# First copies of q and k on VectorE, and a new step order, in a one-core attention and two-layer kernel

## The chip, the cores and the metric

The kernel runs on one core of one Trainium2 chip. The time is that of the device for one execution, in microseconds (us); each kernel's figure is the median of several runs.

## The reference

```python
scores = scale * np.matmul(q, k.transpose(0, 1, 3, 2))   # q, k, v: 2 x 12 heads x 448 x 64
scores = np.where(np.triu(np.ones((448, 448), bool), k=1), -1e9, scores)
scores = scores - scores.max(-1, keepdims=True)
attn = np.exp(scores)
attn = attn / (attn.sum(-1, keepdims=True) + 1e-9)
x = np.matmul(attn, v)              # then heads side by side: x is 896 x 768
h = x @ w_in                        # 768 x 2048
x = np.maximum(0.01 * h, h) @ w_out # 2048 x 768
xn = x / np.sqrt(np.mean(x * x, -1, keepdims=True) + 1e-6) * rms_g
g, val = xn @ w_gate, xn @ w_val    # 768 x 1536 each
out = (g / (1 + np.exp(-g)) * val) @ w_out2
```

## The kernel before

The first 97 us or so are the attention, the rest is a long row of matrix products of the two layers. The attention works on 12 pairs of heads. For each pair p the steps are, by their names in the table `ORDER`: load k and q (`k`, `q`), turn them with TensorE (`tk`, `tq`, lines 306 and 309), take them out of PSUM in a high part (`hk`, `hq`, line 315) and a low part (`lk`, `lq`, line 319), multiply scores (`s`, line 345: blocks 0, 1, 4, 5, then 2, 3, then the tail block 6), take the mask and the row peak (`m`, line 354, VectorE), the exponential (`e`, line 363, ScalarE), guard and inverse of the sums (`g`, `i`), normalise (`n`, line 376), turn the probabilities (`t`, line 383), copy them out (`c`, line 396), multiply by the values (`x`, line 405) and copy the result out in two parts (`f`, lines 413 and 415).

Pair 0 is handled in pieces: its q and k come in chunks a, b and c, are turned on line 269, copied on line 275 and multiplied in plain float32 (line 331, steps `s0.0` to `s0.6`). The q chunks of pair 0 are loaded by DMAs that ScalarE's own queue issues (line 263); all other loads go through SP's queue, in the order of the table. `b`, `d` and `v` load the tails of q, of v, and v itself.

`ORDER` is a written list: each engine gets its instructions in that order and works them off in that order. A mark `@A`, `@D` or `@P` says ScalarE, VectorE or GpSimd where a step can be done by more than one; without a mark a copy goes to VectorE and a normalisation to GpSimd. `~3` is three small multiplies on constants (line 516), which do no work of the result. `w` decodes the first weights of the layers, `y` multiplies the first layer's first columns for the first batch already inside the attention, `z` finishes them.

Buffers rotate: four PSUM banks for scores, three for everything that is turned, one for the value product, four tiles for loaded q and k. A step that takes a bank waits until the last reader of the bank's former content is through.

```python
            def copy_part(p, nm, part, eng):
                (ACT.copy if eng == "A" else DVE.tensor_copy)(
                    out=L["F", p][:, 0, at:at + n].bitcast(F32), in_=L["ps" + nm + part, p][:, :n])
```

Of the kernel before, what the change touches and what calls it, by code (L numbers as in the profile page):

```python
# [15 lines left out]
P = 128  # L16
B, H, S, D = 2, 12, 448, 64
# [20 lines left out]


ORDER = """  # L40
k0a q0a k0b q0b k0c q0c k1 q1 b0 tk0a hk0a@A tq0a hq0a@D ~3 s0.0 tk0b hk0b@A tq0b hq0b@D m0.0 m0.1 e0.0 tk0c
hk0c@A ~1 tq0c hq0c@D s0.2 e0.1 tk1 k2 hk1@A m0.3 m0.2 g0.0@D i0.0 s0.4 q2 q3 b2 lk1 tq1 e0.2 e0.3 hq1@A s0.6
m0.5 m0.4 k3 lq1 e0.5 m0.6 g0.2@P e0.4 tk2 ~1 s1.2 hk2@A s1.0 tq2 i0.2 g0.4@D k4 n0.3@P e0.6 i0.4 m1.2 n0.4@P
lk2 s1.6 e1.2 m1.0 m1.4 g0.6@P hq2@A m1.3 i0.6 lq2 e1.4 n0.5@P n0.2@P tq3 t0.1 e1.0 hq3@A c0.1@A m1.6 tk3
n0.6@P s2.0 n0.1@P n0.0@P hk3@A m1.5 m1.1 lq3 d0 q4 lk3 e1.1 e1.3 e1.5 s2.2 m2.4 m2.1 m2.0 t0.0 m2.2 m2.5
c0.0@A m2.3 e1.6 g1.0@D t0.3 t0.2 s2.6 i1.0 c0.3@A tk4 n1.0 n1.6@P e2.3 c0.2@A m2.6 e2.6 e2.4 s3.0 n1.1 hk4@D
m3.4 n1.4@D e2.0 e2.5 s3.2 tq4 m3.0 m3.2 hq4@D lk4 v0 n1.3 t1.3 lq4 e2.2 e3.4 e2.1 n1.2 n1.5@P x0 c1.3@D t1.0
b1 t1.1 g2.0@P e3.0 c1.0@D m3.1 t1.2 q5 k6 k5 f0.0@A c1.1@A c1.2@A m3.5 m3.3 s3.6 q7 w0.0 i2.0 m3.6 tk6 tq5
f0.1 n2.0 e3.5 hk6@A lk6 q6 tk5 s4.0 e3.1 hk5@A hq5@A n2.6@P s4.2 e3.6 e3.2 m4.0 lq5 m4.3 n2.5@P m4.1 n2.4@P x1
n2.3 e3.3 n2.2 n2.1 lk5 m4.4 g3.0@P w0.1@P e4.1 t2.3 t2.0 t2.2 m4.5 e4.0 i3.0 c2.0@D c2.2@D c2.3@A m4.2 s4.6  # L50
t2.1 q8 e4.3 tq7 tq6 f1.0@A hq7@A c2.1@A n3.1 n3.2 n3.0 n3.6@P s5.0 f1.1 e4.2 m4.6 s5.2 e4.6 e4.5 e4.4 x2
n3.4@P n3.3 hq6@D lq6 lq7 n3.5@P m5.0 m5.4 m5.1 t3.0 t3.3 k7 v1 c3.0@A m5.3 g4.0@D s5.6 t3.2 i4.0 c3.3@A e5.4
e5.1 n4.5@D n4.3 m5.5 m5.2 f2.0@A c3.2@D t3.1 n4.1 tk7 c3.1@A hk7@A m5.6 e5.6 d1 n4.4@P e5.2 s6.0 e5.0 e5.5
n4.0 n4.6@P s6.2 f2.1 m6.4 w0.2 e5.3 m6.0 n4.2 x3 lk7 m6.1 t4.3 w0.3 g5.0@P t4.0 c4.3@A i5.0 f3.0@A m6.2 m6.5
k8 w1.0 v2 c4.0@A s6.6 t4.1 n5.6@P n5.3 m6.3 t4.2 n5.2 n5.5@P n5.1 k9 c4.1@D f3.1 e6.5 c4.2@A s7.6 tk8 tq8 s7.0
e6.0 n5.4@P n5.0 w1.1@P m6.6 m7.6 s7.2 e6.4 hq8@D x4 e6.2 q9 hk8@D m7.0 lk8 lq8 e6.3 t5.0 e6.1 e7.0 t5.2 e6.6
m7.3 m7.4 t5.1 s8.6 g6.0@P c5.2@D f4.0@A c5.0@A e7.6 c5.1@A i6.0 t5.3 m7.2 m7.1 m7.5 c5.3@A tq9 tk9 n6.4@P
hk9@A e7.4 f4.1 m8.6 e7.5 s8.0 hq9@D n6.6@P n6.3 m8.0 m8.5 lq9 k11 q10 s8.2 n6.5@P e7.1 e7.2 n6.2 n6.1 n6.0
e8.0 x5 lk9 m8.2 m8.4 t6.3 e7.3 m8.1 g7.0@D f5.0@A i7.0 q11 t6.0 c6.3@A t6.1 c6.0@A e8.1 k10 w0.4 m8.3 n7.4@P
w0.5@P n7.5@P c6.1@A t6.2 c6.2@A e8.3 s9.0 n7.0 f5.1 m9.0 m9.4 e8.6 m9.5 e8.4 s9.2 n7.1 e8.5 e8.2 e9.5 m9.1 x6  # L60
tk11 s9.6 tq10 n7.2 w0.6 m9.3 hq10@A y0.0 tk10 g8.0@P n7.3 hk11@D m9.2 i8.0 lk11 n8.6@P n8.3 y0.1 t7.0 n7.6@P
hk10@A e9.4 c7.0@A lq10 lk10 y0.2 m9.6 t7.2 f6.0@D t7.3 tq11 y0.3 e9.0 e9.6 c7.2@A v3 t7.1 n8.5@D s10.6 c7.3@D
t8.3 n8.1 w1.2 e9.2 hq11@A c7.1@D e9.3 c8.3@A y0.4 lq11 n8.0 n8.2 n8.4@P t8.0 w1.3 t8.1 t8.2 e9.1 c8.1@A c8.0@A
w1.4 m10.6 g9.0@P f6.1 i9.0 y0.5 n9.5@D n9.1 n9.0 s10.0 z0.0 e10.6 c8.2@A m10.1 m10.0 n9.2 n9.3 m10.5 w1.5@A
s10.2 e10.0 m10.4 m10.3 m10.2 x7 f7.0@A s11.2 n9.4@P e10.2 f7.1 e10.1 e10.4 e10.5 w1.6 s11.0 e10.3 m11.3 m11.5
m11.4 g10.0@P x8 n9.6@P i10.0 m11.2 t9.1 t9.0 f8.0@A c9.1@D f8.1 t9.2 y1.0 m11.0 c9.0@D e11.5 n10.1 n10.4@P
n10.0 n10.5@P t9.3 s11.6 n10.6@D m11.1 t10.0 e11.2 e11.4 n10.2 e11.3 c9.2@A e11.1 z0.1 w2.0 y1.1 g11.2@P n10.3
c9.3@D t10.3 e11.0 i11.2 m11.6 n11.3@D g11.4@D t10.2 n11.2@P i11.4 g11.0@P y1.2 e11.6 x9 n11.4@D c10.2@D
g11.6@D c10.0@A n11.5@P w2.1@A c10.3@D f9.0@A i11.6 t11.2 t10.1 c11.2@A c10.1@A n11.6@D t11.3 y1.3 i11.0 f9.1
n11.0@P n11.1@P w2.2 x10 f10.0@A t11.1 t11.0 c11.1@A y1.4 y1.5 c11.0@A w2.3 z0.2 f10.1 c11.3@D x11 z1.0 f11.0@A  # L70
w2.4 f11.1 z1.1 z1.2
"""


# [613 lines left out]
```

## Time and profile before

| | us |
|---|---|
| median of 3 runs | 589.68 (589.5 to 589.83) |
| the profiled execution, its own time | 591.89 |
| span from its first to its last instruction | 590.1 |
| TensorE busy in that span | 585.5 |
| VectorE busy | 390.0 |
| ScalarE busy | 265.9 |
| GpSimd busy | 47.6 |

The profiled execution is a single one; its span is what the trace covers, its own time includes what lies around the span. A busy TensorE is not TensorE at its peak: the ends of its multiplies are modelled, and a multiply that runs at half the clock, or waits inside its pipeline, counts as busy too.

### The profile page before, as it was taken

The numbers are of one execution on the slowest core, as the hardware profiler recorded it, in microseconds if no ns is written. First come the engines' busy times: TensorE is split into PE (matmuls) and PEld (weight loads), VectorE is DVE, ScalarE is ACT, GpSimd is POOL, SyncE is SP. The second block draws the span as 40 slices with busy tenths as digits, with TensorE's granted clock in tenths as the row PEclk, the third lists the DMA queues.
The fourth block names the chain that finished last, engine by engine and source line by source line (L and its number), as shares of the span: only waits on it lengthen the run. The fifth ranks groups of instructions, "written<-read, shape, count | busy, mean of one in ns | idle before, by whom it ended". The sixth has DMA issues, their size and how long they took to land.

```text
span 590.1 us, 8451 instructions
## 1 busy us (share of the span) xinstructions
PE 585.5 (99%) x3267; PEld 533.6 (90%) x3267; DVE 390.0 (66%) x706; ACT 265.9 (45%) x520; POOL 47.6 (8%) x104
## 2 busy tenths in 40 slices
PE   9999999999999999999999999999999999999997
PEld 5878878999999999999999999999999999999997
DVE  5999996766666555655655998788797796850000
ACT  4989894444444434323333743434444444420000
POOL 3465550000000000000000000000000000000000
PEclk9999999999999999999999999999999999999999
DMA  5893413333333333334233354334343351621001
GB/s 133 204 216 80 96 54 107 108 110 109 109 109 111 112 100 98 108 94 139 91 107 111 105 160 139 116 124 147 115 152 120 108 159 55 190 78 41 28 27 41
DMA packets 83448, 65.04 MB, mean 110 GB/s; under 512 B 35536, under 2 KB 80336, under 8 KB 83408
## 3 DMA queue, kind: packets, MB, share of 16 engines
q1 hardware_dynamic: 82448, 64.27, 37.0%
q8 instruction: 26, 0.43, 0.3%
q10 hardware_dynamic: 960, 0.23, 0.2%
q14 instruction: 14, 0.11, 0.1%
HBM read 61.74 MB, written 2.75 MB: 109 GB/s over the span
## 4 chain that ended last, share of the span: by engine, by line
PE 99%; ACTq 0%; ACT 0%; issue 0%
PE mm L545 17%; PE mm L153 10%; PE mm L154 10%; PE mm L155 10%; PE mm L564 7%; PE mm L563 7%; PE mm L562 7%; PE mm L643 5%; PE mm L645 5%; PE mm L644 5%; PE pt L383 4%; PE x L405 4%; PE s L345 4%; PE qk L306 2%; PE s L331 1%; PE mm L422 0%
## 5 line engine op out<-in xcount | busy, mean ns | idle before, releaser
L153 PE MATMUL mm<-a,hi 128*128 128x448 f32 x300 | 109.7, 366 | 0.0
L154 PE MATMUL mm<-a,lo 128*128 128x448 f32 x300 | 109.6, 365 | 0.0
L155 PE MATMUL mm<-a,hi 128*128 128x448 f32 x300 | 109.6, 365 | 0.0
L134 ACT CAST hi<-we 128x768 fp32r<-128x768 f32 (+1 forms) x59 | 48.2, 817 | 132.0 <-PE mm L545 53.9
L140 DVE TENSOR_TENSOR lo<-we,hi 128x768 fp32r<-128x768 f32 (+1 forms) x60 | 56.0, 933 | 64.5 <-ACT hi L134 64.3
L123 DVE SCALAR_TENSOR_TENSOR we<-we,ws 128x768 int32<-128x768 int32 (+1 forms) x70 | 65.4, 935 | 28.5 <-ACT we L112 26.4
L545 PE MATMUL mm<-a,hi 128*128 128x448 f32 x336 | 81.7, 365 | 0.0
L112 ACT ACTIVATE we<-raw 128x768 f32<-128x768 f32 (+1 forms) x68 | 60.3, 888 | 39.4 <-DVE lo L140 26.0
L545 PEld LDWEIGHTS mm<-a,hi 128*128 128x128 f32 x336 | 63.1, 188 | 5.0
L127 DVE SCALAR_TENSOR_TENSOR we<-raw,we 128x768 int32<-128x768 int32 (+1 forms) x70 | 65.1, 931 | 1.4
L562 PE MATMUL mm<-b,hi 128*128 128x448 f32 x168 | 61.4, 365 | 0.0
L564 PE MATMUL mm<-b,lo 128*128 128x448 f32 x168 | 61.4, 365 | 0.0
L563 PE MATMUL mm<-b,hi 128*128 128x448 f32 x168 | 61.4, 365 | 0.0
L153 PEld LDWEIGHTS mm<-a,hi 128*128 128x128 f32 x300 | 56.3, 188 | 4.5
L154 PEld LDWEIGHTS mm<-a,lo 128*128 128x128 f32 x300 | 56.3, 188 | 4.5
L155 PEld LDWEIGHTS mm<-a,hi 128*128 128x128 f32 x300 | 56.3, 188 | 4.5
L545 PE MATMUL mm<-a,lo 128*128 128x448 f32 x168 | 47.7, 365 | 0.0
L363 ACT ACTIVATE p<-p,st 128x256 f32<-128x256 f32 (+3 forms) x84 | 44.2, 538 | 0.9 <-DVE st L354 0.5
L119 DVE TENSOR_SCALAR ws<-raw 128x768 int32<-128x768 uint32 (+1 forms) x70 | 38.0, 543 | 8.0 <-DMA raw<-in_moe_w_gate_dram 3.3
L376 POOL TENSOR_SCALAR p<-p,st 128x256 f32<-128x256 f32 (+3 forms) x76 | 37.6, 513 | 20.1 <-DVE st L372 6.6
L656 DVE COPY o<-mm 128x384 f32<-128x384 f32 x6 | 3.3, 555 | 53.0 <-PE mm L645 53.0
L563 PEld LDWEIGHTS mm<-b,hi 128*128 128x128 f32 x168 | 31.6, 188 | 2.5
(136 smaller groups left out, 944.0 us busy)
## 6 DMA issues: line engine op xcount, KB each, us to landing
raw<-in_moe_w_out_dram SPq DMA_DIRECT2D x24, 768.0 KB, 4.3
raw<-in_moe_w_in_dram SPq DMA_DIRECT2D x16, 768.0 KB, 4.7
raw<-in_moe_w_gate_dram SPq DMA_DIRECT2D x12, 768.0 KB, 4.4
raw<-in_moe_w_val_dram SPq DMA_DIRECT2D x12, 768.0 KB, 4.3
raw<-in_moe_w_out_dram SPq DMA_DIRECT2D x6, 512.0 KB, 3.6
out_dram<-o SPq DMA_DIRECT2D x14, 192.0 KB, 1.9
n<-in_k_dram SPq DMA_DIRECT2D x22, 112.0 KB, 2.8
vn<-in_v_dram SPq DMA_DIRECT2D x12, 192.0 KB, 4.1
```

The lines of the kernel that those rows point to most:

```text
L112: ACT.activation(out=out, in_=src, func=AF.Copy, scale=2.0 ** -112)
L123: DVE.scalar_tensor_tensor(out=L["e"], in0=L["e"], scalar=3, in1=L["s"], op0=ALU.logical_shift_left, op1=ALU.bitwise_or)
L127: DVE.scalar_tensor_tensor(out=L["e"], in0=L["w"][:, :, 1], scalar=-0x80000000, in1=L["e"], op0=ALU.bitwise_and, op1=ALU.bitwise_or)
L134: ACT.copy(out=L["hi"], in_=L["e"].bitcast(F32))
L140: DVE.tensor_tensor(out=L["lo"], in0=L["e"].bitcast(F32), in1=L["hi"].bitcast(F32), op=ALU.subtract)
L153: PE.matmul(ps, wh, ah, start=(i == 0), stop=False)
L154: PE.matmul(ps, wl, ah, start=False, stop=False)
L155: PE.matmul(ps, wh, al, start=False, stop=(i == n - 1))
L545: PE.matmul(pss[b], w, cols(xT[kk], b)[part], start=kk + part == 0 and w is wh, stop=kk == KC - 1 and w is wl)
L562: PE.matmul(pss[b], wh, ah, start=(f == 0), stop=False)
L563: PE.matmul(pss[b], wh, al, start=False, stop=False)
L564: PE.matmul(pss[b], wl, ah, start=False, stop=(f == NF1 - 1))
```

## The change

Only `ORDER` is different. In its first row the step `hk0a`, the copy of k's chunk a, loses the mark `@A` and so goes to VectorE; `hq0a` was on VectorE already. From `s0.0` on the steps are in a new order, with some of the marks different. One of the small multiplies on constants (`~1` ahead of `s1.2`) is gone. Everything else in the program is the same; all line numbers behind the table are lower by one. The diff, cut to the first rows:

```diff
 ORDER = """
-k0a q0a k0b q0b k0c q0c k1 q1 b0 tk0a hk0a@A tq0a hq0a@D ~3 s0.0 tk0b hk0b@A tq0b hq0b@D m0.0 m0.1 e0.0 tk0c
-hk0c@A ~1 tq0c hq0c@D s0.2 e0.1 tk1 k2 hk1@A m0.3 m0.2 g0.0@D i0.0 s0.4 q2 q3 b2 lk1 tq1 e0.2 e0.3 hq1@A s0.6
-m0.5 m0.4 k3 lq1 e0.5 m0.6 g0.2@P e0.4 tk2 ~1 s1.2 hk2@A s1.0 tq2 i0.2 g0.4@D k4 n0.3@P e0.6 i0.4 m1.2 n0.4@P
-lk2 s1.6 e1.2 m1.0 m1.4 g0.6@P hq2@A m1.3 i0.6 lq2 e1.4 n0.5@P n0.2@P tq3 t0.1 e1.0 hq3@A c0.1@A m1.6 tk3
...
+k0a q0a k0b q0b k0c q0c k1 q1 b0 tk0a hk0a tq0a hq0a ~3 s0.0 tk0b hk0b@A tq0b hq0b@D m0.0 m0.1 e0.0 tk0c hk0c@A
+~1 tq0c e0.1 hq0c@D s0.2 tk1 hk1@A m0.2 m0.3 s0.4 g0.0@D tq1 s0.6 q2 e0.3 e0.2 lk1 hq1@A m0.4 e0.4 m0.5 e0.5 k2
+lq1 g0.2@P tq2 hq2@A m0.6 s1.2 i0.2 g0.4@D n0.3@P i0.0 i0.4 k3 s1.0 e0.6 m1.2 n0.2@P n0.5@P n0.4@P tk2 tk3 s1.6
+d0 m1.3 lq2 n0.0@P e1.2 e1.3 m1.1 m1.0 hk2@A m1.5 hk3@A n0.1@P g0.6@P e1.5 t0.1 lk2 b2 m1.4 lk3 q3 m1.6 i0.6
+n0.6@P k4 e1.0 e1.4 s2.6 e1.1 e1.6 q4 m2.6 t0.0 tq3 c0.1@A hq3@D g1.0@D i1.0 n1.6@P s2.0 s2.2 c0.0@A t0.3
...
```

Over the whole list VectorE has 3 large casts of q or k fewer and 1 copy of probabilities fewer, 3 normalisations more and 2 first parts of `f` more.

The first place is the start of VectorE's list. `F_147` is the tile of pair 0 that holds its turned k and q, `qk_145` and `qk_149` are the turned chunks a of k and of q, `qk_162` is chunk b of q. Before:

```order
L498 MEMSET qe_96 128x1536
L275 COPY F_147<-qk_149 128x128
L275 COPY F_147<-qk_162 128x128
L354 ISA p_98,st_165<-s_155,mask_102 128x128
L354 ISA st_165 128x1
```

And of the change:

```order
L497 MEMSET qe_96 128x1536
L274 COPY F_147<-qk_145 128x128
L274 COPY F_147<-qk_149 128x128
L274 COPY F_147<-qk_162 128x128
L353 ISA p_98,st_165<-s_155,mask_102 128x128
```

VectorE's list has one copy more, at its head; the same copy is gone from ScalarE's list, where it stood right behind the load of the activation table.

The second place is TensorE's list from the turned q of pair 1 on; `s<-F 64x448` is `s0.6`, rows of 112 columns are k, of 128 columns q. Before:

```order
L309 MATMUL qk<-ident,qe 128x128
L331 MATMUL s<-F 64x448 x2
L306 MATMUL qk<-ident,n 128x112 x4
L516 LDWEIGHTS const-bfloat16-1.0
L516 MATMUL warm<-const-bfloat16-1.0 128x256
L345 MATMUL s<-F 128x256 x6
L345 MATMUL s<-F 128x128 x6
L345 MATMUL s<-F 128x384 x6
L306 MATMUL qk<-ident,n 128x128 x3
L309 MATMUL qk<-ident,qe 128x128
L345 MATMUL s<-F 128x448 x3
L306 MATMUL qk<-ident,n 128x128 x3
```

And of the change:

```order
L330 MATMUL s<-F 64x448 x2
L305 MATMUL qk<-ident,n 128x128 x3
L308 MATMUL qk<-ident,qe 128x128
L344 MATMUL s<-F 128x256 x6
L344 MATMUL s<-F 128x128 x6
L344 MATMUL s<-F 128x384 x6
L305 MATMUL qk<-ident,n 128x112 x8
L344 MATMUL s<-F 128x448 x3
L382 MATMUL pt<-ident,p 128x128 x4
L344 MATMUL s<-F 128x448 x3
L382 MATMUL pt<-ident,p 128x128 x4
L305 MATMUL qk<-ident,n 128x128 x3
```

Pair 2's q is turned first and its k later, together with pair 3's k; the tail scores of pair 2 (the second `128x448`) moved ahead of its other scores.

The third place is VectorE's list of the change in front of those tail scores. `F_226` is pair 2's tile: the row with 512 columns is `lq2`, that with 448 is `lk2`; `st_260` belongs to pair 1.

```order
L318 TENSOR_TENSOR F_188<-qk_197,F_188 128x512
L353 ISA p_98,st_165<-s_202,mask_tail_103 128x448
...
L353 ISA p_98,st_260<-s_229,mask_102 128x256
L353 ISA p_98,st_260<-s_230,mask_102 128x256
L318 TENSOR_TENSOR F_226<-qk_221,F_226 128x512
L353 ISA p_98,st_260<-s_246,mask_102 128x128
L353 ISA p_98,st_260<-s_245,mask_102 128x128
L353 ISA p_98,st_260<-s_246,mask_102 128x384
L318 TENSOR_TENSOR F_226<-qk_265,F_226 128x448
```

Before, `lk2` stood right behind the first peak of pair 1, ahead of six others and of `lq2`; now it is behind five of those peaks and behind `lq2`.

## Rows read from the trace of the kernel before

**Rows 1.** TensorE's waits: engine, line, what ended them; us, times, longest.

```profile
PE s L331 <- ACT F L275: 0.4, 1, 0.4
```

**Rows 2.** Chain of waits up to 35 us: start, us, engine, tile and line.

```profile
4.64 0.80 PE s L331 x4
...
9.30 1.58 PE s L331 x4
10.88 0.83 PE qk L306 x3
...
11.93 0.92 PE s L331 x4
12.85 0.54 PE qk L306 x4
...
13.49 1.50 PE s L345 x18
15.00 0.48 PE qk L306 x3
...
15.58 0.60 PE s L345 x3
16.18 0.33 PE qk L306 x3
16.51 0.11 PE qk L309
...
17.59 1.41 PE s L345 x18
19.00 1.46 PE pt L383 x12
...
23.94 1.88 PE x L405 x16
```

**Rows 3.** Timeline from 2.9 us: start, us, engine, line, operation, tiles.

```profile
2.94 0.66 PE L269 MATMUL qk<-ident,n 128*128 128x128 f32 x2
...
3.02 1.28 ACT L275 ACT_TABLE_LOAD   x1 [3.02 <-issue]
...
3.39 0.84 PE L516 MATMUL warm<-const-bfloat16-1.0 128*128 128x256 bf16 x3
...
3.63 0.29 DVE L275 COPY F<-qk 128x128 f32<-128x128 f32 x1 [1.18 <-PE qk L269]
```

**Rows 4.** Timeline of VectorE from 12 us.

```profile
12.58 0.69 DVE L319 TENSOR_TENSOR F<-qk,F 128x512 fp32r<-128x512 f32 x1 [0.61 <-ACT F L315]
13.19 0.61 DVE L354 CUSTOM_DVE_ANT_0 p<-s,mask_tail 128x448 f32<-128x448 f32 x1
...
14.08 0.42 DVE L354 CUSTOM_DVE_ANT_0 p<-s,mask 128x256 f32<-128x256 f32 x1
...
14.43 0.62 DVE L319 TENSOR_TENSOR F<-qk,F 128x448 fp32r<-128x448 f32 x1
14.96 0.28 DVE L354 CUSTOM_DVE_ANT_0 p<-s,mask 128x128 f32<-128x128 f32 x1
...
15.17 0.55 DVE L354 CUSTOM_DVE_ANT_0 p<-s,mask 128x384 f32<-128x384 f32 x1
```

**Rows 5.** Costliest groups: the exponentials; busy us, mean ns, idle before.

```profile
L363 ACT ACTIVATE p<-p,st 128x256 f32<-128x256 f32 (+3 forms) x84 | 44.2, 538 | 0.9 <-DVE st L354 0.5
```

**Rows 6.** Timeline of SP's queue from 6.5 us.

```profile
6.64 1.07 SPq L253 DMA_DIRECT2D n<-in_k_dram  x2
7.81 0.97 SPq L253 DMA_DIRECT2D n<-in_q_dram  x2
```

**Rows 7.** Windows: PE, PEld, DVE, ACT, POOL busy us (instructions), clock, DMA.

```profile
40.00:60.00 20.00, 20.00 (x184) 16.32 (x184) 18.79 (x67) 18.83 (x60) 10.92 (x23) 1.00 0.57 115
```

**Rows 8.** Timeline around the value product of pair 8.

```profile
78.51 0.62 DVE L415 TENSOR_TENSOR a<-x,a 128x448 fp32r<-128x448 f32 x1 [0.61 <-ACT a L413]
...
79.24 0.60 PE L405 MATMUL x<-pT,vn 128*64 128x448 f32 x2
```

More of the change, by code (lines that the diff above doesn't have):

```diff
@@ L40 @@
 ORDER = """
-k0a q0a k0b q0b k0c q0c k1 q1 b0 tk0a hk0a@A tq0a hq0a@D ~3 s0.0 tk0b hk0b@A tq0b hq0b@D m0.0 m0.1 e0.0 tk0c
-hk0c@A ~1 tq0c hq0c@D s0.2 e0.1 tk1 k2 hk1@A m0.3 m0.2 g0.0@D i0.0 s0.4 q2 q3 b2 lk1 tq1 e0.2 e0.3 hq1@A s0.6
-m0.5 m0.4 k3 lq1 e0.5 m0.6 g0.2@P e0.4 tk2 ~1 s1.2 hk2@A s1.0 tq2 i0.2 g0.4@D k4 n0.3@P e0.6 i0.4 m1.2 n0.4@P
-lk2 s1.6 e1.2 m1.0 m1.4 g0.6@P hq2@A m1.3 i0.6 lq2 e1.4 n0.5@P n0.2@P tq3 t0.1 e1.0 hq3@A c0.1@A m1.6 tk3
-n0.6@P s2.0 n0.1@P n0.0@P hk3@A m1.5 m1.1 lq3 d0 q4 lk3 e1.1 e1.3 e1.5 s2.2 m2.4 m2.1 m2.0 t0.0 m2.2 m2.5
@@ L46 @@
[L46 to L70, printed above, removed]
@@ L71 @@
-w2.4 f11.1 z1.1 z1.2
+k0a q0a k0b q0b k0c q0c k1 q1 b0 tk0a hk0a tq0a hq0a ~3 s0.0 tk0b hk0b@A tq0b hq0b@D m0.0 m0.1 e0.0 tk0c hk0c@A
[3 more added lines that the diff above has]
+n0.6@P k4 e1.0 e1.4 s2.6 e1.1 e1.6 q4 m2.6 t0.0 tq3 c0.1@A hq3@D g1.0@D i1.0 n1.6@P s2.0 s2.2 c0.0@A t0.3
@@ new lines @@
+c0.3@A m2.0 lq3 v0 t0.2 m2.4 c0.2@A m2.5 t1.3 tq4 tk4 m2.1 m2.2 n1.2 e2.0 n1.0 m2.3 n1.4@D hk4@D s3.0 s3.2
+n1.5@P n1.1 n1.3 k5 e2.5 e2.1 e2.3 hq4@A m3.3 lq4 m3.2 m3.0 lk4 x0 q5 k6 e2.6 c1.3@A t1.1 t1.2 e2.2 m3.4 e2.4
+g2.0@D c1.2@D f0.0@A t1.0 s3.6 m3.1 c1.1@A c1.0@A tk6 tk5 m3.5 tq5 m3.6 i2.0 f0.1 e3.0 e3.5 e3.1 e3.6 hq5@A
+s4.0 q7 n2.3 n2.4@P n2.0 e3.4 hk5@A s4.2 x1 hk6@D m4.4 lk6 w0.0 m4.2 lk5 b1 n2.2 n2.6@P n2.5@P n2.1 lq5 q6 e3.3
+m4.0 t2.3 k7 f1.0@D v1 q8 e4.2 e3.2 g3.0@P t2.1 c2.3@A t2.2 c2.1@A i3.0 m4.5 s4.6 c2.2@A e4.4 m4.3 t2.0 tq7 tq6
@@ new lines @@
+f1.1 n3.3 m4.1 s5.0 m4.6 hq7@A c2.0@A n3.4@P n3.6@P lq7 m5.4 m5.5 hq6@A s5.2 e4.5 e4.1 n3.5@P e4.3 x2 w0.1@P
+n3.2 e5.4 m5.0 lq6 m5.2 f2.0@D n3.0 e4.6 m5.3 t3.2 t3.3 e4.0 n3.1 c3.3@A tk7 s5.6 g4.0@P c3.2@D i4.0 m5.1 f2.1
+m5.6 t3.1 t3.0 n4.0 n4.3 e5.2 c3.1@D s6.0 n4.4@P n4.5@P s6.2 m6.0 w0.2 n4.1 e5.0 e5.1 n4.2 c3.0@A hk7@A x3
+n4.6@P e5.5 m6.2 lk7 t4.2 m6.4 e5.3 e5.6 t4.3 g5.0@P i5.0 s7.6 t4.0 e6.0 f3.0@A m6.3 m6.5 c4.2@A n5.6@P c4.3@A
+t4.1 k8 n5.0 n5.2 n5.3 e6.3 m6.1 f3.1 c4.0@D c4.1@A e6.4 s6.6 tq8 t5.3 e6.2 e6.5 hq8@A w0.3 tk8 s7.0 m7.6 m6.6
@@ new lines @@
+w0.4 m7.0 s7.2 x4 m7.2 lq8 n5.4@P e6.6 hk8@A e6.1 n5.5@P lk8 k9 q9 v2 n5.1 g6.0@P w1.0 k10 m7.1 i6.0 m7.4 t5.0
+e7.2 c5.3@A n6.3 e7.6 c5.0@D n6.6@P w0.5@P t5.1 e7.0 q10 t5.2 c5.1@A d1 f4.0@A e7.1 c5.2@D s8.6 t6.3 tq9 tk9
+m7.5 m7.3 n6.1 m8.6 f4.1 c6.3@A s8.0 n6.4@P n6.2 hk9@A n6.5@P s8.2 e7.4 e7.5 w1.1@P x5 hq9@A k11 m8.5 lk9 e7.3
+lq9 m8.2 g7.0@P n6.0 f5.0@A t6.2 m8.1 i7.0 n7.0 n7.5@P n7.2 n7.3 t6.0 t6.1 c6.2@A e8.1 c6.1@A e8.2 m8.4 m8.0
+m8.3 c6.0@D f5.1 w0.6 s9.0 e8.6 e8.5 s9.2 x6 e8.4 e8.0 n7.4@P e8.3 tk10 m9.0 m9.5 m9.4 m9.1 tk11 e9.1 n7.1 s9.6
@@ new lines @@
+y0.0 e9.5 tq10 n7.6@P g8.0@P hk11@A hk10@D hq10@A m9.2 i8.0 lk10 q11 y0.1 t7.3 n8.6@D lk11 t7.0 c7.3@A lq10
+y0.2 n8.1 n8.2 n8.3 tq11 t7.1 c7.0@A e9.0 f6.0@D w1.2 m9.6 m9.3 f6.1 y0.3 t7.2 s10.6 e9.2 hq11@A y0.4 lq11 w1.3
+v3 m10.6 c7.1@A e9.3 t8.3 y0.5 e9.6 e9.4 z0.0 s10.0 w1.4 g9.0@P c8.3@A n8.0 n8.4@P n8.5@P s10.2 c7.2@D e10.6
+w1.5@A i9.0 x7 m10.3 m10.4 e10.4 m10.0 f7.0@A t8.2 n9.1 n9.3 m10.5 n9.0 t8.0 t8.1 n9.2 m10.2 m10.1 n9.4@D f7.1
+e10.2 n9.5@P c8.0@D c8.2@A w1.6 s11.0 c8.1@A e10.5 m11.4 m11.5 m11.1 e10.1 e10.3 e10.0 s11.2 x8 g10.0@D n9.6@D
@@ new lines @@
+t9.1 e11.1 i10.0 m11.0 t9.2 f8.0@A s11.6 c9.1@D m11.2 n10.3 n10.5@P n10.4@D m11.3 e11.5 n10.0 c9.2@A e11.0 f8.1
+t9.0 y1.0 t9.3 g11.0@P e11.3 y1.1 c9.0@D w2.0 e11.2 m11.6 i11.0 e11.6 g11.2@D n10.2 n10.6@P c9.3@D i11.2 t10.1
+e11.4 g11.6@D t10.3 y1.2 x9 w2.1@A c10.1@A i11.6 f9.0@A n10.1 n11.2@D c10.3@D t10.2 t10.0 g11.4@D w2.2 n11.6@D
+c10.2@A n11.0@D f9.1 i11.4 n11.3@D t11.3 y1.3 c10.0@A n11.1@D n11.4@D w2.3 n11.5@P x10 z0.1 c11.3@A f10.0@A
+t11.1 t11.2 t11.0 z0.2 c11.1@D f10.1 c11.2@A c11.0@A y1.4 y1.5 x11 f11.0@A z1.0 z1.1 w2.4 z1.2 f11.1
```

## The prediction

> **What bounds the kernel now.** I read the table of TensorE's waits first. From the first scores to the end it has one row, 0.4 us, ended by ScalarE's copy [rows 1]. The chain of waits says the same by time: from 4.64 us on it is TensorE alone, one block behind the other [rows 2]. So the time is the start of that chain plus the TensorE blocks in a row, plus whatever holes hide in the blocks' lengths; those are found by comparing blocks of one form.
>
> Three transposes of a q set (L306) take 0.83 us at 10.88 and 0.33 us at 16.18 [rows 2]. That is the clock: the profile grants TensorE the full share (1.00) wherever it records it [rows 7], but the same instructions run at half the pace until about 11.9 us, which is the lower level (1.2 GHz), and at the upper (2.4 GHz) from then on. Behind 12 us I take as the price of a block the shortest that its form shows: 18 score multiplies 1.41, three wide scores 0.60, a q set 0.33 and 0.11 for its fourth transpose. Full-array work right behind scores or values costs 0.15 more (0.48 against 0.33 for a q set at 15.00 and 16.18); without that turn a k set is 0.39 (0.54 at 12.85), and twelve probability transposes of 1.46 are 0.44 for each four [rows 2].
>
> **The start.** Step s0.0 needs both first copies. VectorE's began at 3.63 and took 0.29, done at 3.92; ScalarE's could begin only at 4.30, behind its table load of 1.28 us that started at 3.02 [rows 3], and s0.0 started at 4.64 [rows 2]. On VectorE the k copy can start once the transpose of 2.94 is through, and VectorE was idle for 1.18 us ahead of 3.63 [rows 3]. Best case: the q copy still starts at 3.63 and both are done at 3.92. Worst: both stand behind 3.63 and end at 4.21 (3.63 + 2 x 0.29). Also ahead of s0.0 are three warm multiplies that start at 3.39 and end, as modelled, at 4.23; a following row starts 0.21 before such an end (3.39 against 2.94 + 0.66) [rows 3], so they leave TensorE at 4.02. I take 4.03 for s0.0, nearest to the row in which the copies do not collide: **a gain of 0.61**, with 0.37 (start at 4.27) as the lower bound. The table load stays, hidden behind VectorE's copies and s0.0.
>
> **From s0.0 to the second pair.** The TensorE rows are the same up to s0.6, so all moves by 0.61 up to the end of the q transposes: 11.93 becomes 11.32. The rise of the clock was at about 11.9, and I hold it there. s0.6 took 0.92 at the upper level; from 11.32 to 11.94 it gets half of 0.62 done, 0.31, and the other 0.61 end it at 12.55 against 12.85: half of the gain is left, 0.30. If the rise moved along with the work, 0.31 more would be kept; one trace cannot tell.
>
> By the Trainium skill (TensorE: Matmul & The Clock Gate, Part 1 on the HAM clock gate) the lower level is the default, activity releases it, and the monitor runs freely instead of starting anew with a kernel. By that rule the rise has no reason to follow s0.0 by the same 0.61, and the sum is the one that holds it; this trace shows one rise and can neither confirm nor refute it.
>
> Next comes the q set of pair 2 instead of the k set and one warm multiply: 0.15 + 0.44 = 0.59 against 0.64 (12.85 to 13.49) [rows 2]. So s1.2 can start at 13.14, not 13.49. Its last input, VectorE's low part of q (lq1), started at 12.58 and took 0.69, ending 0.22 ahead of the scores at 13.49 [rows 2, 4]; 0.61 earlier it is ready for TensorE at 12.88, so there is no wait. The block of 1.50 had a hole of 0.09 that I drop: it ends at 14.55. Two k sets follow (0.54 + 0.39), s1.6 (0.60) and t0.1 (0.44): 16.52.
>
> **The new wait.** s2.6 now stands here, ahead of s2.0, and needs VectorE's low part of k of pair 2 (lk2). On VectorE stand ahead of that, from the start of lq1 at 11.97, by start-to-start times [rows 4]: lq1 0.61, m0.6 with its three small ones 0.89 and one small one more, 0.09 ((0.89 - 0.61) / 3), two 256-wide peaks at 0.35, lq2 0.61, two 128-wide at 0.21, one 384-wide 0.55: 15.84. ScalarE must also have cast k2: behind the q transposes that end at 13.14 it has a cast, three exponentials of 0.54 in the mean [rows 5] and that cast; a cast is bounded by VectorE's 0.62 on the same width [rows 4], which gives 13.14 + 0.62 + 1.62 + 0.62 = 16.00. Then 0.62 for lk2 and 0.22 to hand over: 16.8. **A wait of 0.28**; between nothing, if ScalarE's casts are shorter, and 0.8, if one more exponential gets ahead.
>
> From 16.80 by the same prices: s2.6 0.60, t0.0 0.44, q set 0.44, s2.0 and s2.2 1.41, t0.3 and t0.2 1.03, t1.3 0.44, the q and k sets of pair 4 0.83, s3.0 and s3.2 1.41: 23.40. A second wait, t1.3 for the bank that lq3 frees, behind a cast that VectorE takes over, I set at 0.08; from nothing to 0.4. So x0 starts at 23.48 against 23.94 [rows 2], **0.46 earlier**, with the same set of blocks done in both orders.
>
> **The queues.** On SP the q load of pair 2 takes the place of its k load, issued at 6.64, and k2 that of q2, at 7.81 [rows 6]. Needed at 12.55 and 14.55, both have nearly 6 us and more from issue to use, the span that k2 had before (6.64 to 12.85), in which TensorE did not wait for it. The loads behind them I set at nothing for that reason; a late one would hold its transposes, and all of TensorE behind them, for what it is late.
>
> **Behind x0** both orders do the same TensorE work. No wait shows there before, and the turns of 0.15 are as many (one from scores less, one from values more). In the step list VectorE gets three large casts and one copy-out less, three normalisations and two copies of x more; these nearly cancel, as all are passes over 128 to 512 columns. So 0.46 is carried to the end unless a new wait arises.
>
> The sum against the profiled execution: its span 590.1 becomes 589.64, its own time 591.89 becomes 591.43. The median of the runs shown, 589.68, lies 2.21 below that execution's time, so I forecast **589.2 us**, with 588.5 (no new wait, the rise moves along: 0.36 + 0.31 less) to 590.0 (both waits at their bounds, 0.84 more) as its own range.
>
> **Rivals.**
> *The clock rises earlier.* With the hole in front of s0.0 closed, TensorE is used more densely before 8 us. Were the rise at the start of s0.4, then of its 1.58 us and the 1.05 of the q set (10.88 to 11.93) [rows 2] half would go, 1.3 us, and the 0.31 above: 587.6 if all came through, up to 588.4 where VectorE and ScalarE, which set lk2, give half back. For it: the level stayed low although multiplies ran, so density counts. Against it: the same rows in the same order only shift. Chance 0.10.
>
> *It does not reach the end.* ScalarE and VectorE are each busy for 94% of 40 to 60 us [rows 7]; if they take the 0.46 back in one or two places, 589.6 to 590.2. Chance 0.20.
>
> *Slower: values wait for copies.* The value product has one PSUM bank, so each x waits for VectorE's low part of the one before. For x8 that ended at 79.13 (78.51 + 0.62) and x8 started at 79.24 [rows 8]: margin 0.1. If nine later products each waited 0.3 longer, 2.7 - 0.46 = 2.2 us would be lost: 591.9. It decides (over 0.2% lost) from 1.18 + 0.46 = 1.64 us, 0.18 for each of nine. Against it: no such wait exists before, and filler multiplies of the first layer stand between the late ones. Chance 0.12, most of it near 591.
>
> **How the numbers follow.** A measurement of this kernel tells about 0.2% (1.18 us) from no change. Forecast 0.58, not reaching the end 0.20, early clock 0.10, slower 0.12. Same is the first two less 0.02 for their outer edges: 0.76; faster 0.11 and slower 0.13 take one of these hundredths each. The range may leave out 0.2: 588.2 to 590.7 cuts most of the early clock and most of the slower case.
>
> **What would show it.** In the changed profile s0.0 should start near 4.0 with no ScalarE wait in front, s0.6 should take longer than 0.92, s2.6 should follow t0.1 after a hole of some 0.3 us, x0 should start near 23.5, and the attention's last value product end 0.5 us earlier. I am wrong on the start if VectorE's second copy ends after 4.2; on the clock if transpose sets of 0.33 us appear before 11; on the end if TensorE's table of waits gets rows from VectorE or ScalarE behind 24 us.

## The result, and the profile after

The changed kernel takes 594.74 us (median of 7 runs, 592.91 to 597.37), the kernel before in the same series 589.63 (7 runs): a ratio of 1.006, 95% interval 1.0037 to 1.0082. It is slower by more than can be told from no change, and lies above the whole range of the prediction. The ratios here are taken from runs not over 1.5% above the fastest of their kernel (three further down fall out of them: 599.02, 600.24 and 600.31) and are not the quotient of the two medians, which is 1.0087 here.

The profiled execution of the change has a span of 591.5 us (own time 593.31), 1.4 us more than that of before. It is one of the shorter runs of the change; the median run of 594.74 has no trace. Its table of TensorE's waits, from the first scores to the end:

```profile
PE qk L305 <- ACT p L362: 0.6, 1, 0.6
PE qk L305 <- DMA n<-in_q_dram: 0.5, 1, 0.5
```

The wait of [rows 1] is off this list, two new ones stand on it, both in the attention's first 20 us. From the chain of waits (start us, us, what):

```profile
4.30 0.47 PE s L330 x4
...
7.22 2.62 DMA n<-in_q_dram
9.85 0.14 issue
9.98 0.52 PE qk L305 x3
10.51 0.11 PE qk L308
10.61 1.41 PE s L344 x18
12.03 0.92 PE qk L305 x8
12.94 0.63 PE s L344 x3
13.57 0.44 PE pt L382 x4
14.00 0.74 PE s L344 x3
...
17.78 1.07 ACT pT L395 x2
18.86 0.40 ACT p L362 x2
...
20.27 1.42 PE s L344 x18
21.69 1.88 PE x L404 x16
```

In [rows 2] x0 starts at 23.94, here at 21.69: in spite of both waits the attention is more than 2 us ahead. It still is when it ends: the last value product, x11, starts at 94.83 before and at 92.86 after, and the first pair of multiplies for the inverse root mean square (L588, L589 before) stands at 326.84 and at 324.87, both 1.97 us earlier. Then the lead goes, and 1.4 us with it: 3.4 us are lost between there and the end, where neither table of TensorE's waits has a row.

What is lost is the pace. Two windows of before, TensorE alone (window, us, busy us and multiplies, PEclk, DMA share, GB/s):

```profile
120.00:320.00 200.00, 200.00 (x989) 1.00 0.34 108
330.00:495.00 165.00, 165.00 (x816) 1.00 0.41 130
```

The same two of the change, and the stretch in which the pace is lost:

```profile
120.00:320.00 200.00, 200.00 (x988) 1.00 0.34 107
330.00:495.00 165.00, 165.00 (x800) 1.00 0.41 129
325.00:502.00 177.00, 177.00 (x860) 1.00 0.39 121
```

The same multiplies of 448 columns, TensorE 100% busy in both, granted clock 1.00 in both, and yet 800 of them where 816 stood: 0.2063 us apiece (165/800) instead of 0.2022. The share of busy time hides it; the count shows it, and so do the steps from one start to the next. For the 860 multiplies of the last row that is 860 x 0.0041 = 3.5 us, against the 3.4 us lost. The place where it begins, in the timeline of the change (start us, us, engine, line, tiles):

```profile
323.65 0.37 PE L152 MATMUL mm<-a,hi 128*128 128x448 f32 x1
...
325.07 0.37 PE L588 MATMUL mm<-sl,ones 128*128 128x448 f32 x1
325.28 0.36 PE L152 MATMUL mm<-a,hi 128*128 128x448 f32 x1
...
326.93 0.37 PE L154 MATMUL mm<-a,hi 128*128 128x448 f32 x1
```

From 323.65 to 325.07 there are seven steps from start to start, 0.203 us each; from 325.07 to 326.93 nine, 0.207 each, and so to 502 us. In the trace of before the pair at 326.84 changes nothing.

**What differs ahead of it.** Both kernels enter the layers from x11. The timeline of before there:

```profile
94.53 0.37 PE L424 MATMUL mm<-a,hi 128*128 128x448 f32 x1
94.83 1.83 PE L405 MATMUL x<-pT,vn 128*64 128x448 f32 x12
96.50 0.28 PE L405 MATMUL x<-pT,ve 128*64 128x64 f32 x4
```

The same place in the change:

```profile
92.38 0.37 PE L423 MATMUL mm<-a,hi 128*128 128x448 f32 x1
92.86 1.84 PE L404 MATMUL x<-pT,vn 128*64 128x448 f32 x12
94.49 0.31 PE L404 MATMUL x<-pT,ve 128*64 128x64 f32 x4
```

x11 follows the last filler multiply by 0.30 us before and by 0.48 after. The modelled ends overlap, so the 0.18 us stand in no table of waits, but they are one: x11 needs the bank of the value product, free when `f10.1` on VectorE is done. VectorE in the change:

```profile
89.50 0.61 DVE L147 TENSOR_TENSOR a<-g,a 128x448 fp32r<-128x448 f32 x1
...
90.62 0.96 DVE L122 SCALAR_TENSOR_TENSOR we<-we,ws 128x768 int32<-128x768 int32 x1
91.49 0.68 DVE L395 COPY pT<-pt 128x512 f32<-128x512 f32 x1
92.09 0.61 DVE L414 TENSOR_TENSOR a<-x,a 128x448 fp32r<-128x448 f32 x1
```

`f10.1` (L414) ends at 92.70, behind a copy of probabilities, `c11.1`, that the new order puts ahead of it on VectorE, and x11 starts at 92.86. The late start leaves a mark that is easy to find: the next row, L404 with four multiplies, has 0.31 instead of 0.28.

### The profile page after: what moved, and what is told of

Same layout as the page of the kernel before. It is cut to its first block, busy times and chain, and to the rows that moved or that the text cites. A ratio compares the mean times of both kernels' runs of the same rounds, so it can differ in the third digit from the quotient of the medians.

```text
span 591.5 us, 8453 instructions
## 1 busy us (share of the span) xinstructions
PE 586.0 (99%) x3266; PEld 532.4 (90%) x3266; DVE 390.1 (66%) x709; ACT 266.6 (45%) x521; POOL 46.7 (8%) x100
## 4 chain that ended last, share of the span: by engine, by line
PE 99%; DMA 0%; ACT 0%; issue 0%; ACTq 0%; SPq 0%
PE mm L544 17%; PE mm L152 11%; PE mm L154 10%; PE mm L153 10%; PE mm L561 7%; PE mm L563 7%; PE mm L562 7%; PE mm L643 5%; PE mm L642 5%; PE mm L644 5%; PE x L404 4%; PE s L344 4%; PE pt L382 4%; PE qk L305 1%; PE warm L515 1%; DMA n<-in_q_dram 0%
## 5 line engine op out<-in xcount | busy, mean ns | idle before, releaser
L362 ACT ACTIVATE p<-p,st 128x128 f32<-128x128 f32 (+3 forms) x84 | 44.1, 530 | 1.3 <-DVE st L353 1.2
L563 PEld LDWEIGHTS mm<-b,lo 128*128 128x128 f32 x168 | 31.6, 188 | 2.5
```

What stands on the lines that cost most here:

```text
L563: PE.matmul(pss[b], wl, ah, start=False, stop=(f == NF1 - 1))
```

## The experiments

**The theories.** W: the late start of x11 puts TensorE's multiplies into another step, out of which the 206-ns pace can arise. O: something else of the new order does it. A1: the earlier copy at the start does it. A2: the new order does it, whichever part. A3: the one constant multiply fewer does it. C: what separates the groups of run times that every version has is the time at which the clock rises. Each experiment has 8 to 12 runs of its own, and the kernel before beside it.

**The kernel before, unchanged.**

> The kernel before, word for word, as a second trace of it. In the trace of the change the attention's last value product ended at 94.8 us, 2 us earlier than before, with TensorE's clock at its upper level from 4.4 us instead of 11.9, and yet the span was 1.4 us longer: from 325 us to 502 us every multiply of 448 columns was spaced 206.7 ns instead of 202.7, some 860 times 4 ns, 3.5 us. Theory A (the slow spacing belongs to the change): spacing here 202.7 throughout, median near 589.6, none of five runs above 591. Theory B (the spacing is chance from run to run): some of these runs are 2 to 7 us longer too. Of the clock: if the early rise belongs to the change, it is at about 12 us here again and x0 starts near 24; if it is chance, it may be at 4 to 9 us and x0 2 us earlier.

Measured: 592.02 us, ratio 1.0002 (0.9985 to 1.002). Two of 12 runs are below 589.7, ten at 591.9 to 592.7; 31 runs of the kernel beside it split likewise, 11 to 20, with nothing between 590 and 591.8. So one kernel has two groups 2.7 us apart. The multiplies between 4 and 12 us tell which group an execution is of. The profiled execution of before (columns as in the windows above):

```profile
4.00:12.00 8.00, 7.60 (x31) 1.00 0.66 149
```

The same window of the change:

```profile
4.00:12.00 8.00, 7.47 (x56) 1.00 0.71 161
```

31 multiplies are the lower level (1.2 GHz) to nearly 12 us, 56 the upper (2.4 GHz) from before 5 us. The column of the granted clock has 1.00 in both, so the level is read from the lengths of equal blocks: s0.0 took 0.80 before [rows 2] and 0.47 in the change. Below, an execution or a run is called early or late by this rise. The profiled execution of before, 591.89 us, is a late one; the median of its first runs, 589.68, is of early ones.

**The copy alone.**

```diff
-... tk0a hk0a@A tq0a hq0a@D ~3 s0.0 ...
+... tk0a hk0a tq0a hq0a@D ~3 s0.0 ...
```

> Before, with the first copy of k alone moved from ScalarE to VectorE, order unchanged. If the copy brings the early clock by closing the hole ahead of s0.0: s0.0 at 4.2, rise near 4.4, attention over by some 95 us, and with the spacing of 202.7 kept a median about 2 us under that of a before whose clock rises at 12. If the slow spacing comes with the copy (theory A1): 206.7 in some long stretch and 3 us or more over before. If it comes from the order (A2) or the removed warm multiply (A3): 202.7 throughout.

Measured: 591.02 us, ratio 0.9987 (0.997 to 1.0005), highest run 592.6. s0.0 starts at 4.23 instead of 4.64, 31 multiplies stand between 4 and 12 us, 816 in 330 to 495. The copy does not make the slow pace: A1 falls. Its 0.41 us at the start are too few to be told from nothing. Two of its runs, 591.0 and 591.05, lie between the two groups of before; they have no trace.

**The constant multiply put back into the new order.**

```diff
-lq1 g0.2@P tq2 hq2@A m0.6 s1.2 i0.2 ...
+lq1 g0.2@P tq2 hq2@A m0.6 ~1 s1.2 i0.2 ...
```

> The change, with the one removed multiply on constants put back ahead of s1.2, so that TensorE has as many instructions as before. A3 (the count or place of all later multiplies decides on the spacing): spacing back at 202.7, median at or under 589.6. A1 or A2: 206.7 in a long stretch as in the change, median 592 to 597.

Measured: 592.76 us, ratio 1.0021 (0.9991 to 1.005); three runs at 589.1 to 589.4, six at 592.5 to 592.9, and 597.31, 597.34, 600.31. The profiled one is a run of 597.31; its windows:

```profile
120.00:320.00 200.00, 200.00 (x970) 1.00 0.33 106
330.00:495.00 165.00, 165.00 (x800) 1.00 0.40 125
```

Here the slow pace holds in both windows, and the run is 8 us longer than its fastest. 405 us of layers at 2% more are 8 us. So A3 falls, and the slow pace has two places to begin: at x11, or at the first L588.

**The copy back on ScalarE, the new order kept.**

```diff
-... tk0a hk0a tq0a hq0a ~3 s0.0 ...
+... tk0a hk0a@A tq0a hq0a ~3 s0.0 ...
```

> The change, with the first copy of k back on ScalarE. s0.0 again at 4.6. If the early clock comes from the copy: rise again near 12 us and the attention 1.5 to 2 us longer than in the change. A1 (copy brings the slow spacing): 202.7 throughout, near 589.6. A2 or A3: 206.7 in a long stretch and 593 or more.

Measured: 595.66 us, ratio 1.0071 (1.0031 to 1.0112), 592.2 to 600.0. The trace has 32 multiplies from 4 to 12 us, a late clock, and 800 in 330 to 495. The order does it without the copy. Here, in the trace with the constant multiply put back, and in the two further traces of the new order with its own tail below, x11 starts 0.45 to 0.48 us behind the multiply ahead of it, as in the change.

**The wait at x11 taken out of the new order.** `f10.1` goes ahead of `z0.2` and `c11.1`, and `z0.2` behind x11; all else as in the change.

```diff
-t11.1 t11.2 t11.0 z0.2 c11.1@D f10.1 c11.2@A c11.0@A y1.4 y1.5 x11 f11.0@A z1.0 z1.1 w2.4 z1.2 f11.1
+t11.1 t11.2 t11.0 f10.1 c11.1@D c11.2@A c11.0@A y1.4 y1.5 x11 z0.2 f11.0@A z1.0 z1.1 w2.4 z1.2 f11.1
```

> The change, with the low part of x10 (f10.1) and the last copy of probabilities ahead of z0.2 on VectorE, so that the last value product x11 has its inputs before TensorE comes to it. In the three traces of the new order so far x11 started after a wait (465 to 478 ns behind the multiply ahead, in the old order 297), its paired multiplies stood 35 ns apart instead of 6, and the spacing of 206.7 followed, at once or from the first L588 on. Theory W (the wait at x11 lets TensorE enter the layers out of step): no wait, pairs 6 ns apart, 202.7 throughout, and all runs in 589.0 to 592.9, as clock early or late. Theory O (something else of the new order): 206.7 again in a stretch and runs at 593 to 600.

Measured: 589.27 us, ratio 0.9978 (0.996 to 0.9995); ten of 12 runs in 589.0 to 589.5, the other two 590.87 and 591.98. VectorE and then TensorE at the place:

```profile
90.64 0.62 DVE L414 TENSOR_TENSOR a<-x,a 128x448 fp32r<-128x448 f32 x1
91.17 0.68 DVE L395 COPY pT<-pt 128x512 f32<-128x512 f32 x1
```

```profile
91.94 0.37 PE L423 MATMUL mm<-a,hi 128*128 128x448 f32 x1
92.23 1.84 PE L404 MATMUL x<-pT,vn 128*64 128x448 f32 x12
93.90 0.28 PE L404 MATMUL x<-pT,ve 128*64 128x64 f32 x4
```

`f10.1` is done at 91.26, 0.97 us ahead of x11; the step is 0.29 and the row 0.28, as before, and 816 multiplies stand in 330 to 495:

```profile
330.00:495.00 165.00, 165.00 (x816) 1.00 0.41 129
```

Two steps in another place of VectorE's list bring the median from 596.47 (the change again in the same series, below) to 589.27.

**The wait put into the old order.** A step of weight decoding goes ahead of x11's last copy on VectorE.

```diff
-... w2.3 z0.2 f10.1 c11.3@D x11 z1.0 f11.0@A
-w2.4 f11.1 z1.1 z1.2
+... w2.3 z0.2 f10.1 w2.4 c11.3@D x11 z1.0 f11.0@A
+f11.1 z1.1 z1.2
```

> Before, with one more decoding step of the second weights (0.95 us on VectorE) ahead of the last copy of probabilities, so that x11 has to wait some 0.7 us. Theory W: pairs of x11 35 ns apart, 206.7 in a long stretch in part of the runs, so some of twelve at 593 or more, up to 601. Theory O: 202.7 throughout, and only the wait's 0.7 us: 589.9 to 593.5.

Measured: 592.93 us, ratio 1.0024 (0.9998 to 1.0051): 590.1 to 590.5 five times, 592.6 once, 593.2 to 593.7 four times, 596.4 and 596.6. The interval of the ratio takes in no change. The wait by itself makes a run some 0.7 us longer: the five lowest lie that much above the early group of before, and its late group would lie at 592.6 to 593.5. So the five runs from 592.6 to 593.7 can be late runs with the wait, or early ones with the wait and the slow pace in the last stretch (590.1 to 590.5 and 3.4 more). Only 596.4 and 596.6 cannot: they lie where a late run, the wait and the slow pace add up, and the 108 runs of the unchanged kernel in all series never passed 592.78. That is two of 12, told by their times alone. The profiled one, of 590.52, has the wait and not the pace (816 multiplies in 330 to 495):

```profile
92.41 0.37 PE L424 MATMUL mm<-a,hi 128*128 128x448 f32 x1
93.44 1.84 PE L405 MATMUL x<-pT,vn 128*64 128x448 f32 x12 [0.66 <-ACT g L218]
95.08 0.31 PE L405 MATMUL x<-pT,ve 128*64 128x64 f32 x4
```

The table names ScalarE for the 0.66 us, but by VectorE's timeline it is the moved decoding: the copy that x11 needs came behind it and ended at 93.29 (92.61 + 0.68). So the times speak for the wait as what makes the slow pace possible in the old order too; it does not make it certain, and no trace shows the pace there.

**The mended tail, with a denser start.** Three more constant multiplies among the first transposes.

```diff
-... ~3 s0.0 tk0b hk0b@A tq0b hq0b@D m0.0 m0.1 e0.0 tk0c hk0c@A
-~1 tq0c e0.1 hq0c@D s0.2 ...
+... ~3 s0.0 tk0b hk0b@A tq0b ~1 hq0b@D m0.0 m0.1 e0.0 tk0c hk0c@A
+~2 tq0c ~1 e0.1 hq0c@D s0.2 ...
```

> As e5, with three more small multiplies on constants among the first transposes of pair 0. Six traces have the clock rise at 4.4, 5.2 (first copy on VectorE) or 11.8 to 13.1 (four, one of them with the copy on VectorE), and runs of the old order fall in two groups, 589.2 to 589.9 and 591.9 to 592.8. Theory C (the groups are the clock, early or late, and denser work before 8 us makes early more frequent): most of the runs here in the lower group, near 589.3, fewer than one in four near 592. If the groups are not the clock: as e5, both groups alike.

Measured: 589.50 us, ratio 0.9974 (0.9958 to 0.9991), all 12 runs in 589.09 to 589.86. Neither the late group nor a run of the slow pace is left. This version beats both kernels, the one before by 0.26%: 35 runs of before beside it have 20 at 591.9 to 592.8.

**The changed kernel again.**

> The change itself again, as a second trace, on the same chip as the three others. Theory W: x11 waits, pairs 35 ns apart, 206.7 from 95 or from 325 us to 502, 592.6 or more in nearly all runs: early clock with the last stretch slow 592.9, late with it 595.6, all slow 597.3 or 600. Chance alone: as many runs at 589.3 as the old order has, one in three.

Measured: 596.47 us, ratio 1.0063 (1.0032 to 1.0093), 589.38 to 600.24. The profiled run was the one of 589.38, and it corrected the theory: x11 is late in it as well, by the same rows,

```profile
91.86 0.37 PE L423 MATMUL mm<-a,hi 128*128 128x448 f32 x1
92.31 1.84 PE L404 MATMUL x<-pT,vn 128*64 128x448 f32 x12
93.95 0.31 PE L404 MATMUL x<-pT,ve 128*64 128x64 f32 x4
```

but 816 multiplies stand in 330 to 495:

```profile
330.00:495.00 165.00, 165.00 (x816) 1.00 0.41 129
```

With the wait there, it differs from run to run of one kernel whether the slow pace begins.

**The old order with the copy and the denser start**, to part the clock from the order.

```diff
-... tk0a hk0a@A tq0a hq0a@D ~3 s0.0 tk0b hk0b@A tq0b hq0b@D m0.0 m0.1 e0.0 tk0c
-hk0c@A ~1 tq0c hq0c@D s0.2 ...
+... tk0a hk0a tq0a hq0a@D ~3 s0.0 tk0b hk0b@A tq0b ~1 hq0b@D m0.0 m0.1 e0.0 tk0c
+hk0c@A ~2 tq0c ~1 hq0c@D s0.2 ...
```

> The old order with the k copy on VectorE and three more constant multiplies among the first copies and transposes. Theory (the start decides when the clock rises, the wait ahead of the last value product decides the spacing, and the two are separate): the clock rises between 4 and 6 us in every run, all runs lie in 588.9 to 590.1 with none near 592, and the spacing is 202.7 ns to the end, so the old order gains as much from a dense start as the new one. Rival (the early rise needs the new order of pairs 1 and 2, the multiplies alone do not bring it): runs stay in two groups, two thirds of them at 591.9 to 592.8.

Measured: 589.66 us, ratio 0.9981 (0.9962 to 1.0); eleven of 12 in 589.3 to 590.0, against 8 of 23 of the kernel before beside it. Its row from 4 to 12 us:

```profile
4.00:12.00 8.00, 8.00 (x55) 1.00 0.67 152
```

The dense start brings the early clock without the new order. One run, 593.16, fits no group of the old order. It lies where an early run with the slow pace in the last stretch would (589.7 and 3.4 more), though x11 follows without a wait in the trace of this kernel (0.30 us). It was not profiled, so whether the pace can arise without the wait stays open.

**The new order with the denser start**, its tail as it is.

```diff
-... tq0b hq0b@D m0.0 m0.1 e0.0 tk0c hk0c@A
-~1 tq0c e0.1 hq0c@D s0.2 ...
+... tq0b ~1 hq0b@D m0.0 m0.1 e0.0 tk0c hk0c@A
+~2 tq0c ~1 e0.1 hq0c@D s0.2 ...
```

> The new order as it is, its last steps unchanged, with the three constant multiplies. Theory: the clock always rises early, so the late groups (595.5 to 596, near 600) are gone, but the wait ahead of the last value product stays, so runs spread over about 589.5, 592.9 and 597.3, most of them above 592, median 592 to 597. Rival (a dense start alone also mends the slow spacing): all runs in 589 to 590, as with the mended tail.

Measured: 593.04 us, ratio 1.0035 (1.0006 to 1.0064): 589.4 and 589.8, seven at 592.6 to 593.3, 597.6, and two at 596.3 that were not expected. The profiled run, of 593.26, has 58 multiplies from 4 to 12 us, 988 in 120 to 320 and 800 in 330 to 495: early clock, slow pace from the first L588 on. A dense start does not mend the pace, so the two causes are separate.

All runs together, by whether x11 waits:

| kernels | runs | above 593.0 us | above 594.0 us |
|---|---|---|---|
| no wait: before (96 beside the others, 12 of its own), copy alone, both mended tails, old order with dense start | 156 | 1 | 0 |
| wait: the change twice, its three variants with its tail, old order with the wait | 63 | 35 | 25 |

Between 593 and 594 a run can also be late with a long wait, as in the old order with the wait; above 594 neither clock nor wait reaches. Early runs that are slow in the last stretch alone, such as the traced ones of 593.26 and 593.31, stay below 594, so the last column counts fewer than there are.

## Why the prediction was wrong

**The start.** 0.41 us, not 0.61 (predicted bound 0.37). VectorE's two copies ran from 3.49 to 4.00 (one of them ended at 3.92 before [rows 3]), and s0.0 followed 0.23 later, at 4.23. Too short were the term for the second copy and that for the step from the copies to s0.0 (3.92 to 4.03, 0.11 us). The row with the lower bound was the nearer one.

**The clock.** "I hold it there" (at 11.9) did not hold in this execution, and the time of the rise is no constant of the kernel at all. The rise came before 5 us, the rival "the clock rises earlier", and brought more than I priced: x0 at 21.69 instead of 23.48. But the old order can have the same early rise. The kernel with the wait at x11 put into the old order has the start of before word for word; its trace, from 4 to 12 us and at x0:

```profile
4.00:12.00 8.00, 7.04 (x53) 1.00 0.67 151
21.85 1.88 PE x L405 x16
```

So with the clock early in both, the new order is 0.16 ahead at x0, not 0.46, and the rest of the 2.25 us is the clock. Whether the new order makes an early rise more frequent was not tested by itself; ten of 12 runs with the mended tail, against 15 of 35 of before beside them, point that way. A step behind it does not hold either: "the median of the runs shown lies 2.21 below that execution's time". I took for an offset what was the distance of two groups, and set a sum for a late execution against a median of early ones. The Trainium skill (TensorE: Matmul & The Clock Gate, Part 1) says that the monitor runs freely and that the same kernel can leave the lower level at different points; the two groups of one kernel, 589.5 and 592.3, agree. It holds the cost of the rise to be under 1% of a span: what a late rise costs over an early one, 2.7 of 590 us or 0.5%, lies within that, and is more than the change was to bring.

**The waits of the first 20 us.** s2.6 waited about 0.14 (0.74 against 0.60), not 0.28, in an execution with an early clock. With the clock up early the load of q2 was needed at 9.5 us and not at 12.5: it was issued at 7.2, landed at 9.85, and cost 0.5, where I set it at nothing. The second wait, t1.3 for the bank that lq3 frees, did not come: the twelve probability transposes that end with t1.3 run without a hole. The q set of pair 4 behind them waited 0.6 instead, for ScalarE, which I had not priced:

```profile
17.09 1.54 PE L382 MATMUL pt<-ident,p 128*128 128x128 f32 x12
19.25 0.52 PE L305 MATMUL qk<-ident,n 128*128 128x128 f32 x3 [0.62 <-ACT p L362]
```

The early clock outweighed all of them: at the end of the attention this execution is 1.97 us ahead of the late one of before.

**Behind x0.** That "both orders do the same TensorE work", and that "0.46 is carried to the end unless a new wait arises", is the step that failed. The wait did arise, and where the slower rival put it: a value product waiting for `f` of the one before. I priced nine of 0.3 us from the margin of [rows 8]; there is one of 0.18, by my own working too small to decide anything. What decided was behind it: a multiply of the layers does not always cost the same, and after such an entry it can cost 4 ns more, 860 times or, through 405 us, some 1,960 times. In the traced execution that took back the whole lead of 1.97 us and 1.4 us more. No row of before shows the second pace, so its price could not be read there; but the chance of 0.13 for "slower" rested on waits alone. With no slow pace and an early clock in both, judged by the run times, the new order does bring a part of the 0.46: its ten early runs with the mended tail have a median of 589.26, the 15 early ones of before beside them 589.55, 0.29 less.

**What is shown and what is not.** Shown: in the traced executions the loss is the pace (steps and counts at equal clock and equal busy share). Of the 51 runs of the new order with its own tail 23 pass 594 us; with two steps of VectorE moved so that x11 does not wait, no run of 24 passes 592. Copy, constant multiply and clock are not the cause. Shown by times alone: the wait put into the old order brings two of 12 runs that the old order does not have. Not shown: what inside TensorE holds the second pace, why it begins at x11, at the first L588 or not at all with the same late start, why the longer wait in the old order brings it less often than the short one in the new, and whether it can begin without a wait (the run of 593.16).

## What to carry to other kernels

Where TensorE is full, count its multiplies in equal windows as well as reading its waits: a pace that is 2% slower shows as 100% busy. Let nothing that a long dense stretch waits for stand behind deferrable work on another engine, even if the wait is a fifth of a microsecond. And before a profiled execution is set against a median, look whether the runs fall into groups, and which one the profile is of.

## What the hardware showed that was not expected

Two paces of the same stream of 448-column multiplies with their weight loads at one granted clock: 0.2022 us (816 in 165 us) and 0.2063 (800), each held for 165 us and more. The Trainium skill (TensorE: Matmul & The Clock Gate, Back-to-back issue gap) has weight loads and multiplies set the spacing of such a stream together; its formula for a multiply by itself, N/2.4 + 2.5, would make it 189 ns here by estimate, and it says that a stream at large N goes below that. No run here does: both paces are above.

The rise of the clock comes in two groups, with 30 to 32 or 53 to 58 multiplies between 4 and 12 us in the twelve traces and no case between. The run times of the unchanged kernel split likewise, 2.7 us apart; three runs of two other versions (591.0, 591.05 and 590.87) lie between, without a trace. Three more constant multiplies among the first transposes left only the early one in 12 of 12 runs with the mended tail.
